# A decode step (attention over a cache, then two small MLP blocks): VectorE's branch removed, one store of four rows, last matrix in pieces of 5, 6, 2 and 1 parts, and the residual's bias prepared earlier

## The chip, the cores and the metric

The kernel runs on one core of a Trainium2 chip. The metric is the device time of one execution in microseconds (us), less is better. The core has five engines that run their own instruction streams side by side: TensorE (PE in the profile; its weight loads are PEld), VectorE (DVE), ScalarE (ACT), GpSimd (POOL) and SyncE (SP). SP and ACT also issue transfers (DMA), which sixteen DMA engines carry out. Engines wait for each other and for transfers through semaphores.

## What is computed

One token of batch 1 with width D = 512 passes an attention over a cache of 16384 positions, with 32 query heads and 8 key/value heads, and then a block B. The reference, cut to what matters:

```python
x = A_x
h = x + _A_ref(_layernorm(x, axis=-1), A_k_cache, A_v_cache, A_wq, A_wo)
h2 = h + _B_ref(_layernorm(h, axis=-1), B_w1, B_w2, B_w3, B_w4)

def _B_ref(x, w1, w2, w3, w4):            # S = 1 here
    h = _gelu(_layernorm(x, axis=-1) @ w1)
    ...                                   # h's four quarters shifted along the sequence by one or two places
    x1 = x + hs
    h2 = _gelu(_layernorm(x1, axis=-1) @ w3) @ w4
    return x1 + h2
```

The sequence has length one, so a shift along it leaves zeros: hs is zero and x1 = x. What remains of block B is a layernorm, w3 (512 x 1792), a gelu, w4 (1792 x 512) and two additions. Because the input of B is itself a layernorm of h, the output is

h + r (h - mean) + gelu(r' (h - mean) @ w3) @ w4

with r the inverse root of the layernorm and r' that of the two layernorms in a row.

## The kernel before

The kernel is written without a scheduler. Each operation is recorded by a helper (`pe`, `dve`, `act`, `pool`, or `P.op` directly) into the list of its engine with the keys it reads (`r`) and writes (`w`); `Program.op` derives the dependences, and `Program.emit` writes each engine's list out in the order in which it was recorded, with a semaphore wait in front of an operation whose dependence is on another engine or a transfer. `emit` calls `_run` for SP, ACT and POOL, `_vector` for VectorE and `_tensor` for TensorE. So the order of the text is the order on each engine.

An operation without a function (`dve(None, ...)`, `pe(None)`) marks a place. `_vector` puts a hint for a branch at VectorE's start (L146), sets a register to 0 (L147), runs the list up to the marked place, waits for what the mark depends on, and issues there a branch that is taken if the register is below zero (L154), which it never is. `_tensor` runs TensorE's list in loops and has such a hint (L221) and a never-taken branch (L336) of its own, at `pe(None)` inside the last matrix.

Transfers are issued on SP by `load` (L458), in this order: wq; four pairs of heads with two key halves (`kb`) of 4 MB and a value tile (`vb`) of 8 MB each; then the matrices of the end. Keys and values are loaded while the pair before is worked on; the matrices of the end take the place of the last key halves, wo in `kb[0]`, w3 and w4 in `kb[1]`. SP issues a load as soon as the tile it overwrites is free.

The end runs as follows. `o_b` (L751) is the attention's output. wo is multiplied as 32 rows r_ (L757) in three pieces, `WO = ((0, 16), (16, 28), (28, 32))`. Ahead of the second piece stand six dummy matmuls, `unread(6)` (L498), whose result nobody reads. `osum` (L762) and `row_sums` give h (`hr`), its square (into `xs`, L518), its transpose `hT`, and on TensorE minus the mean and minus the mean square, which VectorE copies into columns 0 and 1 of the state tile `s` (L524). ACT makes `hc`, the centred h (L771). TensorE multiplies w3 in two pieces (L777) and runs four dummy matmuls. Meanwhile the two inverse roots are iterated, r' on VectorE with `kw` made on ACT (L552), r on POOL (L554 to L560); POOL adds 1 to r in column 13 (L785). Two gelus on ACT (L788) and two transposes on VectorE (L792) give `hcol`, 14 columns. The first transpose also waits for the first piece of w4.

ACT writes the residual into the PSUM bank `h_ps` (L799): `hr` times column 13 plus the bias in column 12, where column 12 is minus the mean times r (L797). TensorE adds the product with w4 on top (L805): 14 parts m with four matmuls each, of 32 columns of weights side by side. w4 comes in four transfers:

```python
W4 = ((0, 4), (4, 9), (9, 13), (13, 14))
```

Part m waits for the transfer that holds it. Finally ACT copies `h_ps` to `fin` (L810), which holds the four quarters of the output row on partitions 0, 32, 64 and 96, and two transfers write it out, two rows each, one issued by SP and one by ACT (L814); SP's last instruction (L816) waits for both.

Of the kernel before, what the change touches and what calls it, by code (L numbers as in the profile page):

```python
# [10 lines left out]
ACTF = mybir.ActivationFunctionType  # L11
# [13 lines left out]
class Program:  # L25
# [69 lines left out]
    def emit(self):  # L95
        for ops in self.ops.values():
            for o in ops:
                for d in o.deps:
                    d.needed = True
        told = {self.place(o) for e in ("PE", "DVE") for o in self.ops[e] if o.needed and o.at}  # L100
        for e in ("PE", "DVE"):
            for o in self.ops[e]:
                o.needed = o.needed or (o.at is not None and self.place(o) in told)
        for e, ops in self.ops.items():
            sems, n = {}, {}
            for o in ops:
                if o.dma is None and o.needed:
                    if o.own not in sems:
                        name = f"e_{e}" if o.own is None else f"e_{e}_{o.own}"
                        sems[o.own] = self.ctx.enter_context(self.nc.semaphore(name))  # L110
                    n[o.own] = n.get(o.own, 0) + o.worth
                    o.sem, o.val = sems[o.own], n[o.own]
        self.nc.switch_bb("body", parent=None)
        for e, eng in (("SP", self.nc.sync), ("ACT", self.nc.scalar), ("POOL", self.nc.gpsimd)):
            self._run(eng, self.ops[e], {})
        self._vector()
        self._tensor()

    @staticmethod
# [15 lines left out]
    def _run(self, eng, ops, have):  # L135
        for o in ops:
# [2 lines left out]
                    eng.wait_ge(s, v)  # L139
                    have[i] = v  # L140
            self._issue(eng, o)

    def _vector(self):
        eng = self.nc.vector
        rv = eng.alloc_register("never")
        hint = eng.mark_branch_hint_location()  # L146
        eng.reg_mov(rv, 0)  # L147
        ops, seen = self.ops["DVE"], {}
        on = next(n for n, o in enumerate(ops) if o.fn is None)
        self._run(eng, ops[:on], seen)  # L150
        for s, v, _ in self._wants(ops[on]).values():
            eng.wait_ge(s, v)

        eng.br_lt(rv, 0, "body", "ve_on").branch_hint(hint)  # L154
        self.nc.switch_bb("ve_on", parent=None)
        self._run(eng, ops[on + 1:], seen)

    def _tensor(self):
        nc, eng, ops = self.nc, self.nc.tensor, self.ops["PE"]
# [191 lines left out]
WO = ((0, 16), (16, 28), (28, 32))  # L351
VP = 2
W3 = ((0, 2), (2, 4))
W4 = ((0, 4), (4, 9), (9, 13), (13, 14))
PAIRS = HKV // 2
RPARTS = 6
QPAD = 4 * 7
# [10 lines left out]
def bass_sequential_preLN__gqa_block_cached__mixer_s_mlp__decode_kernel(  # L368
# [13 lines left out]
    with ExitStack() as ctx:  # L382
        sb = lambda name, shape, dt: ctx.enter_context(nc.sbuf_tensor(name, shape, dt))
        ps = lambda name, shape, dt: ctx.enter_context(nc.psum_tensor(name, shape, dt))
        P = Program(nc, ctx)
# [36 lines left out]
        bias = sb("bias", [128, 1], FP32)  # L422
# [9 lines left out]
        hr = sb("hr", [128, 128], FP32)  # L432
# [50 lines left out]
        def dve(fn, r=(), w=(), bank=()):  # L483
            return P.op("DVE", fn, r, w, bank)

        def act(fn, r=(), w=(), bank=()):
            return P.op("ACT", fn, r, w, bank)
# [8 lines left out]
        def unread(times):  # L496
            field = qb[:, :, :, :].rearrange("p a j q -> p (a j q)")
            P.op("PE", lambda e: e.matmul(O_ps[1][:, :], field[:, 0:128], field[:, 0:512], start=True, stop=True),  # L498
                 r=["qb"], bank=[("O", 1)], times=times)
# [253 lines left out]
        for r_ in range(32):  # L753
            q = r_ % 4
            if r_ == WO[1][0]:
                unread(6)
            pe(lambda e, r_=r_, q=q: e.matmul(O_ps[0][32 * q:32 * q + 32, :], copies(o_b[:, r_:r_ + 1], 32),  # L757
                                              wo_sb[:, r_ * D:(r_ + 1) * D], start=(r_ < 4), stop=(r_ >= 28)),
               r=["o_b"] + [("r", 0, n) for n in (piece(WO, r_),) if n], w=[("O", 0)], bank=[("O", 0)])
# [8 lines left out]
        s = st[1]  # L768
# [6 lines left out]
        for k in range(NCH):  # L775
            for q in range(4):
                pe(lambda e, k=k, q=q: e.matmul(s_ps[32 * q:32 * q + 32, 0, 0:FQ], hc[:, k, :],  # L777
                                                w3_sb[:, k, q * FQ:(q + 1) * FQ], start=(k == 0), stop=(k == NCH - 1)),
                   r=["hc"] + [("r", 1, n) for n in (piece(W3, k),) if n], w=[("s", 0)], bank=[("s", 0)])
        unread(4)  # L780
        variances(1, (0, 1))
        seeds(1, (0, 1))
        inverse_root(1, 1, dve, act)
# [2 lines left out]
        for n in range(2):  # L786
# [5 lines left out]
            dve(lambda e, lo=lo, hi=hi: e.transpose(  # L792
                hcol[:, lo:hi, :].rearrange("p m u -> p (m u)"),
                hg[:, :].rearrange("p (i m) -> p m i", m=NHC)[:, lo:hi, :]), r=[("hg", n)] + [("r", 1, len(W3))] * (n == 0), w=[("hcol", n)])
        dve(None, r=[("r", 1, len(W3) + 1)])

        act(lambda e: e.activation(s[:, 12:13], s[:, 0:1], ACTF.Identity, scale=s[:, 6:7]),  # L797
            r=[(S, 0), (S, 6)], w=[(S, 12)])
        act(lambda e: e.activation(h_ps[:, 0:128], hr[:, :], ACTF.Identity, bias=s[:, 12:13], scale=s[:, 13:14]),  # L799
            r=["hr", (S, 12), (S, 13), ("hcol", 0)], w=[hkey], bank=[hkey])  # L800
        for m in range(NHC):
            if m == W4[1][0]:
                pe(None)
# [4 lines left out]
                   r=[("hcol", 1)] * (2 * m >= NHC) + [("r", 1, len(W3) + n) for n in (piece(W4, m),) if n],  # L808
                   w=[hkey], bank=[hkey], also=[("hcol", 0)] * (2 * m < NHC))
        act(lambda e: e.activation(fin[:, :], h_ps[:, 0:128], ACTF.Identity), r=[hkey], w=["fin"], bank=[hkey])  # L810

        rows = out[0, 0:1, :].rearrange("o (q j) -> (o q) j", q=4)
        for n, by in enumerate(("SP", "ACT")):
            P.op(by, lambda e, n=n: e.dma_start(rows[2 * n:2 * n + 2, :], fin[64 * n:64 * n + 64:32, :]),  # L814
                 r=["fin"], w=[("out", n)], dma=f"out{n}")
        P.op("SP", lambda e: e.nop(), r=[("out", 0), ("out", 1)])  # L816
        P.emit()

    return nc
# [28 lines left out]
```

## Time and profile before

| what | value |
|---|---|
| median of three runs | 190.89 us (190.88 to 191.0) |
| the profiled execution | 190.97 us |
| its span, first to last instruction | 189.53 us |
| bytes read from HBM | 79.17 MB, 418 GB/s over the span |
| busy: PE, DVE, ACT, POOL | 68%, 62%, 8%, 4% of the span |
| mean granted clock of TensorE | 0.887 |

The profile is of one execution. Its parts are the busy times, the span in slices, the DMA queues, the chain of work that ended last (followed back from the last instruction to what released each step), groups of equal instructions with their mean duration and what ended the idle time before them, and the transfers with the time from issue to landing. In a timeline a row gives the start in us, the duration in us, the engine (SPq and ACTq are the issuing sides of SP and ACT), the line, the operation, the tile written and the tiles read, the shapes and the number of instructions merged into the row; in brackets stands the idle time of the engine before it and what ended it. In a row of a DMA queue stand the packets, the MB and the share of the time of sixteen engines. The records behind these views also have each packet's start and each transfer's landing to the nanosecond.

### The profile page before, as it was taken

The page shows a single profiled execution, that of the slowest core. Times are in us where ns is not written, and L with a number is a line of the kernel's source. Part 1 is how long each engine was busy: PE and PEld are TensorE (multiplying, and loading weights), DVE is VectorE, ACT ScalarE, POOL GpSimd, SP SyncE. Part 2 cuts the span into 40 slices and gives each one's busy share as a digit, 9 for nine tenths or more (in the row PEclk, how much of TensorE's full clock was granted, in tenths as well). Part 3 has the DMA queues.
Part 4 walks back from the last instruction along what each step waited for, and adds up shares of the span by engine and source line. Part 5 has one row for each costly group of instructions (what it writes and reads, how often), then busy time and mean ns, then how long its engine had stood idle before and what let it go on. Part 6 is the DMA issues. An engine that isn't in the chain of part 4 may idle for free.

```text
span 189.5 us, 2371 instructions
## 1 busy us (share of the span) xinstructions
PE 128.4 (68%) x743; PEld 48.0 (25%) x743; DVE 117.6 (62%) x151; ACT 14.4 (8%) x23; POOL 6.7 (4%) x15
## 2 busy tenths in 40 slices
PE   0109709996980498968703979696539996974874
PEld 0103203442230133322301423223113332231222
DVE  6740799995523989945038989460469896614270
ACT  3000200000400000004000000040000000500031
POOL 7100000000000000000000000000000000000040
PEclk9999985899999579996995899996978999998755
DMA  6999999999899999997999999999999989999992
GB/s 222 443 443 443 443 443 443 443 443 443 367 415 436 443 553 443 443 443 325 422 443 394 422 429 443 443 443 443 443 436 422 443 387 422 436 429 415 414 410 108
DMA packets 3330, 79.20 MB, mean 418 GB/s; under 512 B 384, under 2 KB 512, under 8 KB 1280
## 3 DMA queue, kind: packets, MB, share of 16 engines
q1 hardware_dynamic: 3316, 79.17, 97.5%
q8 instruction: 1, 0.02, 0.0%
q14 instruction: 1, 0.01, 0.0%
q10 hardware_dynamic: 12, 0.00, 0.0%
HBM read 79.17 MB, written 0.00 MB: 418 GB/s over the span
## 4 chain that ended last, share of the span: by engine, by line
DMA 66%; DVE 15%; PE 14%; issue 3%; SPq 1%; ACT 0%; DVEq 0%
DMA kb<-in_A_k_cache_dram 45%; DMA kb<-in_B_w_dram 14%; DVE kt L635 14%; PE banks L646 9%; DMA vb<-in_A_wq_dram 6%; PE banks L612 5%; SPq L458 1%; DVE qcol L619 1%; PE banks L805 0%; DVE qb L626 0%; DVE xn L603 0%; ACT fin L810 0%; SPq L139 0%; DVEq L139 0%; DVE qn L720 0%
## 5 line engine op out<-in xcount | busy, mean ns | idle before, releaser
L646 PE MATMUL banks<-kt,qn 128*128 x256 | 69.5, 415 | 25.3 <-DVE kt L635 23.9
L635 DVE STREAM_TRANSPOSE kt<-kb 128x2048 int32<-128x2048 int32 (+1 forms) x37 | 71.3, 1989 | 10.0 <-DMA kb<-in_A_k_cache_dram 8.4
L646 PEld LDWEIGHTS banks<-kt,qn 128*128 x256 | 26.3, 103 | 67.9 <-issue 51.8
L498 PE MATMUL banks<-qb 128*128 128x512 bf16 x58 | 22.3, 462 | 0.4
L686 PE MATMUL banks<-vb,pt 128*32 128x512 bf16 x256 | 16.4, 412 | 3.6 <-POOLq L473 2.9
L671 ACT ACTIVATE p_sb<-banks,bias 128x1024 bf16<-128x1024 f32 x4 | 4.5, 1114 | 132.6 <-DVE nmh L667 132.6
L702 DVE TENSOR_SCALAR od<-banks,rowc 128x128 f32<-128x128 f32 x4 | 1.4, 351 | 19.1 <-PE banks L686 19.1
L675 DVE STREAM_TRANSPOSE pt<-p_sb 64x1024 bf16<-64x1024 bf16 x8 | 9.9, 1239 | 5.4 <-ACT p_sb L671 5.3
L612 PE MATMUL banks<-vb,xn 128*128 x32 | 8.7, 440 | 6.1 <-DVE xn L603 6.1
L660 DVE TENSOR_REDUCE mx<-banks 128x1 f32<-128x1024 f32 x4 | 4.9, 1224 | 8.0 <-PE banks L646 8.0
L686 PEld LDWEIGHTS banks<-vb,pt 128*32 128x32 bf16 x256 | 7.0, 103 | 11.2 <-POOLq L473 3.1
L498 PEld LDWEIGHTS banks<-qb 128*128 128x128 bf16 x58 | 5.8, 104 | 15.4 <-issue 15.2
L619 DVE STREAM_TRANSPOSE qcol<-banks 64x1024 f32<-64x1024 f32 x4 | 4.8, 1227 | 6.9 <-PE banks L612 6.9
L554 POOL TENSOR_SCALAR st<-st 128x1 f32<-128x1 f32 x1 | 0.2, 246 | 175.9 <-DVE st L534 175.9
L663 PE MATMUL banks<-mxd,mean 128*128 128x128 f32 x8 | 2.0, 326 | 6.6 <-DVE mxd L661 6.6
L612 PEld LDWEIGHTS banks<-vb,xn 128*128 128x128 bf16 x32 | 3.5, 110 | 10.9 <-issue 8.3
L708 PE MATMUL banks<-od,zo 128*32 128x128 f32 x8 | 1.6, 285 | 6.5 <-DVE od L705 6.5
L655 ACT ACTIVATE banks<-mean 128x1024 f32<-128x1024 f32 x4 | 4.1, 1027 | 18.7 <-DVE qcol L619 18.6
L705 DVE SCALAR_TENSOR_TENSOR od<-banks,rowc,od 128x128 f32<-128x128 f32 x12 | 4.2, 350 | 0.4
L579 PE MATMUL banks<-x,quarter 4*128 4x128 bf16 x1 | 0.3, 284 | 6.0 <-DVE quarter L577 6.0
L576 DVE CAST ident<-ident_f 4x4 bf16<-4x4 f32 x1 | 3.8, 3848 | 0.6 <-POOL ident_f L571 0.6
L762 DVE COPY osum<-banks 128x256 f32<-128x256 f32 x2 | 0.8, 420 | 5.2 <-PE banks L757 5.2
(77 smaller groups left out, 45.6 us busy)
## 6 DMA issues: line engine op xcount, KB each, us to landing
kb<-in_A_k_cache_dram SPq DMA_DIRECT2D x8, 4096.0 KB, 29.7
vb<-in_A_v_cache_dram SPq DMA_DIRECT2D x2, 4096.0 KB, 29.5
vb<-in_A_wq_dram SPq DMA_DIRECT2D x1, 4096.0 KB, 12.2
kb<-in_A_wo_dram SPq DMA_DIRECT2D x1, 2048.0 KB, 25.0
kb<-in_B_w_dram SPq DMA_DIRECT2D x2, 896.0 KB, 23.2
kb<-in_A_wo_dram SPq DMA_DIRECT2D x1, 1536.0 KB, 28.3
kb<-in_B_w_dram SPq DMA_DIRECT2D x2, 512.0 KB, 25.9
kb<-in_B_w_dram SPq DMA_DIRECT2D x1, 640.0 KB, 26.0
```

Of the source, the lines that this page charges most:

```text
L498: P.op("PE", lambda e: e.matmul(O_ps[1][:, :], field[:, 0:128], field[:, 0:512], start=True, stop=True), r=["qb"], bank=[("O", 1)], times= ...
L576: dve(lambda e: e.tensor_copy(ident[:, :], ident_f[0:4, 0:4]), r=["ident_f"], w=["ident"])
L612: pe(lambda e, k=k: e.matmul(row[:, bass.ds(P.b + P.b0, 512)], copies(xn[:, k:k + 1], 128), wq_k[:, k, bass.ds(P.c + P.c0, REP * DH)], sta ...
L619: dve(lambda e, g=g, b=b, half=half: e.transpose(qcol[64 * g:64 * g + 64, 2 * b:2 * b + 2, :, :].rearrange("p e m u -> p (e m u)"), half.r ...
L635: P.op("DVE", lambda e, view=view: e.transpose(view(kt), view(kb[y])), r=[("r", y, i) for i in range(RPARTS)], w=[("kt", t + i) for i in r ...
L646: pe(lambda e, n=n: e.matmul(row[:, bass.ds(P.y, 512)], qn[:, n, bass.ds(P.q, 128)], key_piece(P.k, n), start=False, stop=(n == 3), skip_g ...
L655: act(lambda e: e.activation(s_all, copies(mean4[:, 0:1], 1024), ACTF.Identity, scale=0.0), r=["mean4", "p"], w=[("s", 0), ("s", 1)], **both)
L660: dve(lambda e: e.tensor_reduce(mx[:, :], s_all, AX.X, ALU.max), r=[("s", 0), ("s", 1)], w=["mx"], **both)
L671: act(lambda e: e.activation(p_sb[:, :], s_all, ACTF.Exp, bias=bias[:, 0:1], scale=float(SCALE), accum_out=acc[:, :]), r=[("s", 0), ("s", ...
L675: dve(lambda e, g=g: e.transpose(pt[64 * g:64 * g + 64, :, :, g, :], p_sb[64 * g:64 * g + 64, :]), r=["p"], w=["pt"])
L686: pe(lambda e, l=l, ct=ct, ch=ch: e.matmul(O_ps[0][32 * ct:32 * ct + 32, :], pt[:, l, ch, :, :].rearrange("p g u -> p (g u)"), tiles[:, l ...
L705: dve(lambda e, block=block, c=c: e.scalar_tensor_tensor(od[:, :], block, rowc[:, c:c + 1], od[:, :], ALU.mult, ALU.add), r=[key, "rowc", ...
```

## The change

VectorE's list is now written out by `_run` like those of SP, ACT and POOL, without hint, register, final wait and branch; TensorE's branch stays, and its mark moves with the first piece of w4 from part 4 to part 5. w4 comes in pieces of 5, 6, 2 and 1 parts in place of 4, 5, 4 and 1. The dummy matmuls ahead of wo's second piece are five in place of six. ACT makes two things between `hc` and `kw`: the mean (column 0 with its sign turned) in column 12, and the centred h in `xs`, which is free by then. The residual is then `xs` times column 13 plus column 12, (h - mean)(1 + r) + mean, the same value as before; the bias no longer depends on r. One transfer on SP stores the four rows of `fin`, and SP's last instruction waits for it.

```diff
@@ emit
-        for e, eng in (("SP", self.nc.sync), ("ACT", self.nc.scalar), ("POOL", self.nc.gpsimd)):
+        for e, eng in (("SP", self.nc.sync), ("ACT", self.nc.scalar), ("POOL", self.nc.gpsimd),
+                       ("DVE", self.nc.vector)):
             self._run(eng, self.ops[e], {})
-        self._vector()
         self._tensor()
@@
-    def _vector(self):
-        eng = self.nc.vector
-        rv = eng.alloc_register("never")
-        hint = eng.mark_branch_hint_location()
-        eng.reg_mov(rv, 0)
-        ops, seen = self.ops["DVE"], {}
-        on = next(n for n, o in enumerate(ops) if o.fn is None)
-        self._run(eng, ops[:on], seen)
-        for s, v, _ in self._wants(ops[on]).values():
-            eng.wait_ge(s, v)
-
-        eng.br_lt(rv, 0, "body", "ve_on").branch_hint(hint)
-        self.nc.switch_bb("ve_on", parent=None)
-        self._run(eng, ops[on + 1:], seen)
@@
-W4 = ((0, 4), (4, 9), (9, 13), (13, 14))
+W4 = ((0, 5), (5, 11), (11, 13), (13, 14))
@@ wo
-                unread(6)
+                unread(5)
@@ behind w3's matmuls
         unread(4)
+        act(lambda e: e.activation(s[:, 12:13], s[:, 0:1], ACTF.Identity, scale=-1.0), r=[(S, 0)], w=[(S, 12)])
+        act(lambda e: e.activation(xs[:, :], hr[:, :], ACTF.Identity, bias=s[:, 0:1], scale=1.0), r=["hr", (S, 0)], w=["xs"])
         variances(1, (0, 1))
@@ behind the transposes
-        dve(None, r=[("r", 1, len(W3) + 1)])
-
-        act(lambda e: e.activation(s[:, 12:13], s[:, 0:1], ACTF.Identity, scale=s[:, 6:7]),
-            r=[(S, 0), (S, 6)], w=[(S, 12)])
-        act(lambda e: e.activation(h_ps[:, 0:128], hr[:, :], ACTF.Identity, bias=s[:, 12:13], scale=s[:, 13:14]),
-            r=["hr", (S, 12), (S, 13), ("hcol", 0)], w=[hkey], bank=[hkey])
+
+        act(lambda e: e.activation(h_ps[:, 0:128], xs[:, :], ACTF.Identity, bias=s[:, 12:13], scale=s[:, 13:14]),
+            r=["xs", (S, 12), (S, 13), ("hcol", 0)], w=[hkey], bank=[hkey])
@@ the store
-        rows = out[0, 0:1, :].rearrange("o (q j) -> (o q) j", q=4)
-        for n, by in enumerate(("SP", "ACT")):
-            P.op(by, lambda e, n=n: e.dma_start(rows[2 * n:2 * n + 2, :], fin[64 * n:64 * n + 64:32, :]),
-                 r=["fin"], w=[("out", n)], dma=f"out{n}")
-        P.op("SP", lambda e: e.nop(), r=[("out", 0), ("out", 1)])
+        P.op("SP", lambda e: e.dma_start(out[0, 0:1, :].rearrange("o (q j) -> (o q) j", q=4), fin[0:128:32, :]),
+             r=["fin"], w=["out"], dma="out")
+        P.op("SP", lambda e: e.nop(), r=["out"])
```

## The prediction

> **What bounds the kernel now.** I read the page's own chain of waits first, then that chain in order of time from 157 us on, then the timeline of the last stage, then the DMA records of two windows, and last the landing of each transfer in the trace.
>
> ```profile
> span 189.5 us, 2371 instructions
> DMA 66%; DVE 15%; PE 14%; issue 3%; SPq 1%; ACT 0%; DVEq 0%
> ```
>
> Two thirds of the chain that ended last is DMA. The records of the window from 2 to 186.4 us, and of the window after it, show why:
>
> ```profile
> q1 hardware_dynamic: 3302, 78.84, 99.6%
> ...
> q8 instruction: 1, 0.02, 1.6%
> q14 instruction: 2, 0.02, 1.1%
> ```
>
> In the first window the sixteen DMA engines are 99.6% busy, with SP's loads and nothing else (it has only that queue). The two instruction queues appear only behind the last weight packet. So no edit ahead of 186 us can gain anything unless it takes bytes off the loads, and any byte put onto a DMA engine is paid at the end. The change can act on the last weights' landing, and on what lies between it and the last instruction. The chain there:
>
> ```profile
> 159.71 26.85 DMA kb<-in_B_w_dram
> 186.56 0.04 issue
> 186.61 0.75 PE banks L805 x20
> 187.36 0.02 issue
> 187.38 0.28 ACT fin L810
> ```
>
> The third piece of w4 (parts 9 to 12) lands at 186.56, then 20 matmuls, then the copy to `fin`. The timeline of the same stretch, with what feeds it:
>
> ```profile
> 177.20 1.25 PE L757 MATMUL banks<-kb,o_b 128*32 128x512 bf16 x16
> ...
> 181.58 0.20 ACT L552 ACTIVATE st<-st 128x1 f32<-128x1 f32 x1
> ...
> 182.79 0.27 DVE L558 TENSOR_SCALAR st<-sti,st 128x1 f32<-128x1 f32 x1
> ...
> 183.94 1.04 DVE L792 STREAM_TRANSPOSE hcol<-hg 128x224 bf16<-128x224 bf16 x2 [0.68 <-ACT hg L788]
> 184.24 0.30 ACT L797 ACTIVATE st<-st 128x1 f32<-128x1 f32 x1
> 184.29 0.23 POOL L785 TENSOR_SCALAR st<-st 128x1 f32<-128x1 f32 x1
> 184.63 0.46 ACT L799 ACTIVATE banks<-hr,st 128x128 f32<-128x128 f32 x1
> 185.15 1.15 PE L805 MATMUL banks<-kb,hcol 128*32 128x128 bf16 x36
> 186.61 0.72 PE L805 MATMUL banks<-kb,hcol 128*32 128x128 bf16 x20 [0.31 <-DMA kb<-in_B_w_dram]
> 187.38 0.28 ACT L810 ACTIVATE fin<-banks 128x128 bf16<-128x128 f32 x1 [2.29 <-PE banks L805]
> 187.68 0.60 SPq L814 DMA_DIRECT2D out_dram<-fin  x1
> 187.69 0.56 ACTq L814 DMA_DIRECT2D out_dram<-fin  x1
> ```
>
> TensorE starts w4 at 185.15 with nine parts in hand and then stands until the third piece comes; ACT and DVE have been done for over a microsecond. The transfers' landings in the trace, in us: wo's second and third pieces 176.73 and 178.00, w3's second 182.38, w4's four 183.67, 185.25, 186.56, 186.84. The stores: SP's, issued 187.684, landed 189.239; ACT's, issued 187.689, landed 189.504; the span ends at 189.527, when SP's wait for the second of them ends. One execution of 190.97 us thus has a span of 189.53 and 1.44 around it; it is 0.08 above the median of 190.89.
>
> **The pieces of w4.** The bytes, the number of transfers (four) and of descriptors stay, so the last part, alone in its piece in both kernels, should land at 186.84 again. Before, 16 matmuls wait for 186.56 and run from 186.608; they go out in groups of eight some 0.107 apart (186.608, 186.689, then 186.796 and 186.903 by the trace), so the last part's four come at 187.009 to 187.019 although it has been there since 186.84. After, only parts 11 and 12, eight matmuls, stand on the third piece, and are out by about 186.70. The last four then start when their own piece lands: 186.84 plus the 0.044 that the first of 186.608 took after 186.564, so 186.884 to 186.895. That is 0.124 earlier, and the first matmuls after a pause take 0.287 where one in a stream takes 0.311 to 0.314, so 0.14 to 0.15. I take 0.14. The second piece now carries parts 5 to 10 and lands some 0.65 ahead of 186.56 (two parts of a piece whose four took 1.31), at 185.91; its 24 matmuls need three groups of eight, 0.32, and are out by 186.3, before the third piece comes. The first piece grows to five parts and lands at 183.67 + 1.58 / 5 = 183.99; VectorE's first transpose waits for it and started at 183.94, so it moves to about 184.03, and the start at 185.15 by less than 0.1. What covers this is the stand of TensorE: 44 matmuls need 0.6, so the start may slip to 186.0. Bounds: 0 if the last piece lands as late as TensorE gets to it now, 0.3 if one dummy matmul less (below) lifts the granted clock, 0.50 over this stretch, and the last 0.31 shrinks by half.
>
> **The one store.** ACT's issue (0.56) goes, and SP's final wait is for one landing in place of two. By SP's own two-row store the landing comes 1.555 after the issue, by ACT's 1.815, and the longer sets the end now: 0.265 less. Four rows have no row of their own as a store; the load of x is four rows of the same 256 bytes: 1.357 after its issue, its rows spread over 0.11 (1.969 to 2.080), where SP's two rows were 0.008 apart. I take SP's row, plus half that spread for two rows more: 1.615, a gain of 0.20. Bounds: 0 (as ACT's) and 0.46 (as the load of x). I stay at the store, since reading and writing ends differ for a load.
>
> **The bias known ahead.** ACT's `activation` of 0.30 at 184.24 behind POOL's 184.20 goes from the late chain; two others come between `hc` (ends 181.47) and `kw` (181.58): about 0.20 as L552 and 0.40 as `hc`. `kw` ends near 182.3 instead of 181.78; VectorE wants it at 182.79 and POOL makes its own. The addition to h_ps still waits for POOL's last value (184.52) and for the first transpose (about 184.55), so it starts at about 184.6 as now. Nothing on the path; without that cover 0.6.
>
> **One dummy matmul less (L498, five for six).** Each is 0.43. TensorE is free 0.4 earlier at 176.8, where wo's second piece has just landed (176.73), but the third comes at 178.00 and starts the last four of wo as now. Worth 0, as the loads set every later start up to w3's second half.
>
> **VectorE's branch.** Gone are the hint (0.05) and the register move (0.04) at 0.75 us, in front of a wait for wq that lands at 12.9, and at 185.28 a wait and a 0.07 branch behind which VectorE does nothing more. TensorE's own branch stays, four matmuls later. As instructions: 0. But two instruction transfers follow the two branches (TensorE's at 185.236, VectorE's at 185.280): 16 KB at 186.483 for 0.927, and 8 KB at 187.120 for 0.307. If the branch or its hint is what held one of them back, it may now go among the loads. Bounds: 0, and the 0.93. I take 0, since VectorE's some 170 instructions go once straight through and no instruction transfer of any engine is seen among the loads; the trace doesn't say whose these two are.
>
> [...]
>
> **Sum.** 190.97 - 0.14 - 0.20 = 190.63; less the 0.08 by which this execution stands above the median, **190.55**, 0.18% below 190.89. A difference of about 0.2%, 0.38 us (190.51, 191.27), is what a measurement of this kernel can tell from no change.
>
> **Rivals.**
> Code among the loads (the slower side). Place: one of the sixteen engines, any time from 2 to 186 us. They never idle, and their order at landing stays from wq (12.42 to 12.92) to the last piece (186.34 to 186.84), so a lag of one engine stays to the end. Price: 16 KB at the loads' pace (4 KB in 0.161 to 0.165) is 0.65, alone it took 0.93. On a middle engine (186.56) that ends 0.37 to 0.65 past 186.84, on the last by all of it: 190.92 to 191.48, say 191.2. It decides from a shift of 0.34 on. For it: both transfers come right behind the two branches. Against: nothing shows that VectorE needs a block; one of 8 KB (0.32) would cost the middle engine 0.04 only.
> A store as quick as x's load, since it no longer shares its issue with another: 0.46 for 0.20, so 190.29. For it: SP's first packet came 1.20 after its issue, x's 0.94. Against: x shared its start with wq's load too.
> Half the gain only: the store's four rows land as late as ACT's two, or TensorE's last four matmuls are as late as now: 190.55 + 0.14 to 0.20, 190.7. Against: the landing at 186.84 and the issue of 187.684 are plain in the trace.
> A change that does less than it says: the piece of parts 11 and 12 is issued before the last one as the third was, so nothing speaks for this beyond the case before.
>
> **How the numbers follow.** Forecast (190.40 to 190.65) 0.46, code among the loads 0.28, quick store 0.15, half the gain 0.11. Faster by over 0.2%, below 190.51: a little under half of the forecast, all of the quick store: 0.38. Slower, above 191.27: somewhat over half of the code case: 0.18. The rest, 0.44, within 0.2%. The range takes in the quick store's better half and the code case up to a middle engine: 190.25 to 191.30, with some 0.04 left below and 0.15 above.
>
> **What would show it.** After: third piece near 186.56 with eight matmuls behind it, last piece 186.84, the last four near 186.88, `fin` near 187.24, SP's issue near 187.55, one landing some 1.6 later, span near 189.19. The code case is wrong if the instruction queues again appear only behind the loads; right if one appears before 186 us and the last landing moves past 186.84. A later start of w4 than 186.0, or a `kw` later than 182.79, would make the covers wrong.

## The result, and the profile after

The changed kernel takes 191.67 us (median of nine runs, 191.24 to 191.81) and the kernel before, in the same comparison, 190.88 (nine runs, 190.55 to 191.07): a ratio of 1.0039, with a 95% interval of 1.0031 to 1.0048. It is 0.79 us slower. 190.55 was predicted, with a range of 190.25 to 191.30.

The profiled execution of the changed kernel took 191.74, 0.77 more than that of before, with 1.42 around its span in place of 1.44. Its page still has DMA as two thirds of the chain that ended last:

```profile
span 190.3 us, 2359 instructions
DMA 66%; DVE 14%; PE 14%; issue 4%; SPq 1%; ACT 0%; DVEq 0%
```

The DMA records from 2 to 186.4 us, the window in which before had SP's queue alone, now have a second row (packets, MB, share of the time of sixteen engines):

```profile
q1 hardware_dynamic: 3284, 78.72, 99.4%
q14 instruction: 1, 0.01, 0.0%
```

The stretch from 52 to 53 us shows what it costs by itself. A packet counts whole in the window in which it starts, so a share can pass 100%; 2.0% of sixteen engines over 1 us is 0.32 us of one engine:

```profile
q1 hardware_dynamic: 16, 0.52, 125.4%
q14 instruction: 1, 0.01, 2.0%
```

The packet records give it to the nanosecond: 8192 bytes at 52.299 us for 0.313. The records don't name a packet's engine, but the transfer starts where one packet ends, and a packet of 32 KB starts at 52.605, where the transfer ends (52.612). It took 1.871, where the others that start from 52 to 53 us take 1.213 to 1.216. So by these times one engine lost 0.31 + 0.66 = 0.97 us. Until then the sixteen engines land a transfer within 0.36 to 0.38 us of each other; from the next landing on within 1.25 to 1.33, up to the third piece of w4 (0.50 to 0.56 all through in before). The first of these landings is at 62.234 in place of 61.417, and each later one is some 0.8 late as well, up to w3 and the third piece of w4 (187.33 where 186.56 was forecast). The engine that lands second to last is where it was (0.01 earlier). So it is one engine that is late, and its lag stays; the records show the engines 99.4% busy, which leaves hardly any idle time to make it up in.

The end of the chain, in order of time (start, duration, what):

```profile
161.01 26.95 DMA kb<-in_B_w_dram
187.96 0.04 issue
188.00 0.33 PE banks L789 x3
188.33 0.02 issue
188.35 0.28 ACT fin L794
```

It is now the last piece of w4, one part, that sets the end, not the third as before; it lands at 187.959 in place of 186.840. That is 1.12 late: 0.8 from the engine's lag, and 0.3 more of its own. The timeline of the same stretch:

```profile
184.88 1.04 DVE L779 STREAM_TRANSPOSE hcol<-hg 128x224 bf16<-128x224 bf16 x2 [0.80 <-DMA kb<-in_B_w_dram]
...
185.57 0.46 ACT L783 ACTIVATE banks<-xs,st 128x128 f32<-128x128 f32 x1 [0.55 <-DVE hcol L779]
...
186.09 0.46 PE L789 MATMUL banks<-kb,hcol 128*32 128x128 bf16 x20 [1.22 <-ACT banks L783]
...
186.75 0.92 PE L789 MATMUL banks<-kb,hcol 128*32 128x128 bf16 x32 [0.20 <-DMA kb<-in_B_w_dram]
...
188.00 0.30 PE L789 MATMUL banks<-kb,hcol 128*32 128x128 bf16 x4 [0.33 <-DMA kb<-in_B_w_dram]
188.35 0.28 ACT L794 ACTIVATE fin<-banks 128x128 bf16<-128x128 f32 x1 [2.32 <-PE banks L789]
188.65 0.63 SPq L795 DMA_DIRECT2D out_dram<-fin  x1
```

The last part has its four matmuls alone behind its landing, as the change intends, and `fin` starts 0.394 after the landing, where before it was 0.542. The store is issued at 188.654 and lands at 190.286, 1.632 later, where before the longer of two took 1.815. The two profiled spans close: +1.12 for the landing, -0.15 for what follows it, -0.18 for the store, together +0.79 (190.318 - 189.527). The clock is about the same in both stretches, 0.50 in before and 0.52 from 188.00 to 188.35 us here.

So the two gains of the forecast stand in this profile nearly as sized (0.14 and 0.20), and over a microsecond of late landing, for which the forecast has 0, outweighs them.

### The profile page after: what moved, and what is told of

The parts are those of the page before. It is cut to its first block, busy times and chain, and to the rows that moved or that the text cites. A ratio compares the mean times of both kernels' runs of the same rounds, so it can differ in the third digit from the quotient of the medians.

```text
span 190.3 us, 2359 instructions
## 1 busy us (share of the span) xinstructions
PE 127.2 (67%) x737; PEld 48.1 (25%) x742; DVE 117.6 (62%) x151; ACT 14.4 (8%) x24; POOL 6.7 (3%) x15
## 4 chain that ended last, share of the span: by engine, by line
DMA 66%; DVE 14%; PE 14%; issue 4%; SPq 1%; ACT 0%; DVEq 0%
DMA kb<-in_A_k_cache_dram 46%; DMA kb<-in_B_w_dram 14%; DVE kt L620 13%; PE banks L631 9%; DMA vb<-in_A_wq_dram 6%; PE banks L597 5%; SPq L443 1%; DVE qcol L604 1%; DVE qb L611 0%; PE banks L789 0%; DVE xn L588 0%; ACT fin L794 0%; SPq L139 0%; DVEq L139 0%; DVE qn L705 0%
## 5 line engine op out<-in xcount | busy, mean ns | idle before, releaser
L631 PE MATMUL banks<-kt,qn 128*128 x256 | 70.7, 427 | 23.2 <-DVE kt L620 22.0
L631 PEld LDWEIGHTS banks<-kt,qn 128*128 x256 | 26.8, 105 | 66.6 <-issue 49.8
L671 PE MATMUL banks<-vb,pt 128*32 128x512 bf16 x256 | 18.0, 441 | 3.6 <-POOLq L458 3.0
L483 PE MATMUL banks<-qb 128*128 128x512 bf16 x52 | 18.5, 388 | 0.5
L742 PE MATMUL banks<-kb,o_b 128*32 128x512 bf16 x32 | 3.0, 487 | 3.3 <-DMA kb<-in_A_wo_dram 2.0
```

The lines of the kernel that those rows point to most:

```text
L631: pe(lambda e, n=n: e.matmul(row[:, bass.ds(P.y, 512)], qn[:, n, bass.ds(P.q, 128)], key_piece(P.k, n), start=False, stop=(n == 3), skip_g ...
L671: pe(lambda e, l=l, ct=ct, ch=ch: e.matmul(O_ps[0][32 * ct:32 * ct + 32, :], pt[:, l, ch, :, :].rearrange("p g u -> p (g u)"), tiles[:, l ...
```

## The experiments

Each kernel was run beside the kernel before on the same chip; in five groups, in which before had medians of 190.80, 190.78, 190.70, 190.61 and 190.67. The span is the mean over a kernel's executions, and so is the time outside the span (before: 189.3 to 189.5, and 1.33 to 1.35).

| kernel | edit | median | ratio [95%] | span | outside |
|---|---|---|---|---|---|
| branch_out | before without VectorE's branch | 191.64 | 1.0043 [1.0031, 1.0055] | 190.23 | 1.35 |
| branch_kept | changed, VectorE's branch kept | 190.87 | 1.0002 [0.9992, 1.0011] | 189.24 | 1.64 |
| no_hint | before, branch kept, hint out | 191.40 | 1.0030 [1.0019, 1.0041] | 190.11 | 1.33 |
| nops20 | changed, 20 empty operations | 191.49 | 1.0035 [1.0022, 1.0047] | 190.16 | 1.33 |
| pad20 | changed, 20 small memsets early, tile in front | 191.31 | 1.0023 [1.0013, 1.0033] | 189.84 | 1.38 |
| two_fetches | changed, 66 memsets, tile in front | 191.23 | 1.0028 [1.0019, 1.0038] | 189.89 | 1.36 |
| two_fetches_b | the same, tile behind | 192.20 | 1.0085 [1.0069, 1.0100] | 190.80 | 1.40 |
| pad_only | changed, unused tile in front | 190.65 | 1.0004 [0.9994, 1.0014] | 189.35 | 1.35 |
| early_mark | before, branch ahead of o_f | 190.88 | 1.0007 [0.9998, 1.0016] | 189.49 | 1.37 |
| late_mark | before, branch behind the last piece | 191.82 | 1.0056 [1.0042, 1.0071] | 189.40 | 2.43 |
| kept_early | branch_kept, branch a piece earlier | 191.57 | 1.0041 [1.0029, 1.0052] | 190.18 | 1.35 |
| two_stores | kept_early with two stores | 190.89 | 1.0011 [1.0003, 1.0020] | 189.57 | 1.35 |
| one_store | before with one store | 190.49 | 0.9988 [0.9980, 0.9997] | 189.18 | 1.34 |
| pieces | before with the new pieces | 190.86 | 1.0013 [1.0003, 1.0023] | 189.45 | 1.50 |
| one_store_five | one_store, third piece cut in two | 190.61 | 1.0000 [0.9991, 1.0009] | 189.34 | 1.33 |
| pad_before | before, unused tile in front | 190.09 | 0.9965 [0.9951, 0.9978] | 188.78 | 1.33 |
| one_store_pad | one_store, unused tile in front | 190.03 | 0.9960 [0.9946, 0.9973] | 188.66 | 1.34 |

### The branch alone, and all but the branch

branch_out does one part of the change alone, the first hunk of its diff with the mark behind the transposes taken out too. branch_kept undoes that part alone. no_hint leaves branch, register and wait in the kernel before and takes out what points ahead to it:

```diff
-        hint = eng.mark_branch_hint_location()
@@
-        eng.br_lt(rv, 0, "body", "ve_on").branch_hint(hint)
+        eng.br_lt(rv, 0, "body", "ve_on")
```

> Kernel before with VectorE's hint, register, final wait and branch taken out, nothing else. Theory (code among the loads): the 8 KB instruction transfer comes near 52 us as in the changed kernel, holds its DMA engine up by about 0.97 us (0.31 for itself, 0.66 for the transfer behind it), the last piece of w4 lands near 187.8 to 188.0 where it landed at 186.84, and the time is before plus 0.9 to 1.1: 191.8 to 192.0. Rival (the store, the pieces or the bias make the changed kernel slower): no instruction transfer ahead of 186 us, 190.9.

> Changed kernel with VectorE's branch left in as before; store, pieces, bias and dummy matmuls as changed. Theory: no instruction transfer ahead of 186 us, last piece near 186.84, the gains of 0.14 (pieces) and 0.2 (store) come through: 190.4 to 190.65. Rival: 191.5 or more.

> Kernel before with the branch left in, but without its hint at the start. If the hint is what holds the code transfer back: 8 KB near 52 us, 191.8 to 192.0. If the branch alone holds it: none ahead of 186 us, 190.9.

The branch alone explains the loss: taking it out costs 0.84 (191.64 to 190.80), keeping it in the changed kernel takes it to 0.07 of before. Its size was a little less than the 0.9 to 1.1 expected of branch_out, and in the execution that was profiled, the shortest of the six (191.15), the last piece landed at 187.36 and not at 187.8 to 188.0. There too the transfer took 0.325 and the packet behind it 1.875. But the spread of the landings was 0.73 to 0.77 ahead of the transfer and is 0.97 behind it, so only about 0.24 of the engine's lag reached the end. How much does reach it depends on where the engine stands among the sixteen: in the changed kernel the spread grows by 0.90 (0.37 to 1.27), in no_hint by all of the 0.97 (0.67 to 1.64). The DMA records from 2 to 186.4 us, of branch_out and then of branch_kept:

```profile
q1 hardware_dynamic: 3285, 78.83, 99.6%
q14 instruction: 1, 0.01, 0.0%
```

```profile
q1 hardware_dynamic: 3297, 78.77, 99.4%
```

The row of q14 is there in the one and missing in the other, so these 8 KB are VectorE's code. no_hint has the transfer too, 8192 bytes at 52.631, and costs 0.60 with the branch still in place (191.40, under the 191.8 to 192.0 expected): it is the hint, near VectorE's start, that keeps the code back (with it the first 8 KB come at 187.120 in before). In every trace here row q14 has exactly two transfers of 8 KB behind 20 us: both from 185.9 us on where hint and branch are kept, and the first among the loads where the hint is gone.

branch_kept shows the second thing that the forecast has wrong. It was expected at 190.4 to 190.65 and came at 190.87. Its span did shrink, by 0.23 (189.24 to 189.47), but the time outside it grew by 0.29. The end of its timeline is as early as the forecast has it:

```profile
185.69 1.58 PE L805 MATMUL banks<-kb,hcol 128*32 128x128 bf16 x56
...
187.32 0.28 ACT L810 ACTIVATE fin<-banks 128x128 bf16<-128x128 f32 x1 [1.68 <-PE banks L805]
187.62 0.62 SPq L811 DMA_DIRECT2D out_dram<-fin  x1
```

Its branch runs at 186.03 where that of before ran at 185.28, since the first two pieces of w4 now hold eleven parts in place of nine. Two code transfers of VectorE follow, at 187.587 and at 190.307, and the execution ends after the second of them. That is taken up below.

### Where in the program the code comes

nops20 put 20 empty operations at VectorE's start, pad20 put 20 real ones (memsets of one column of a tile that nobody reads) ahead of `xn`:

```diff
+        pad = sb("pad", [128, 80], FP32)
@@ ahead of xn
+        for i in range(20):
+            dve(lambda e, i=i: e.memset(pad[:, i:i + 1], 0.0))
```

> Changed kernel with 20 instructions that do nothing at VectorE's start. If the transfer comes when VectorE's instruction count reaches the end of a block of code, it comes 20 instructions earlier: near 22 to 27 us for 52.3, the late engine shows first in the landing of 32 us for that of 61 us, and the time stays at 191.5 to 191.8. If it comes at a fixed time or from another engine: again near 52 us.

> The changed kernel with 20 one-column memsets on VectorE ahead of xn, where it waits for wq. If the transfer comes when VectorE's instruction count reaches a block's end, it comes 20 instructions earlier: 26 to 30 us for 52.3, and the late engine shows from the landing of about 32 us on. If it comes at a fixed time or from another engine: again near 52 us. Time 191.4 to 191.7 in both.

nops20 tells nothing of the place: the trace of VectorE has none of its 20 operations, and its first memset starts at 0.81 as in the changed kernel. So it is a second run of the changed kernel, with the transfer at 52.126; whether the operations are in the program at all the trace doesn't say. In pad20 the transfer came earlier, though not as early as the 26 to 30 us expected. The DMA records from 31 to 32 us have it:

```profile
q14 instruction: 1, 0.01, 1.9%
```

It starts at 31.464. Count VectorE's records in the trace, leaving out the second record of an operation that also reads its accumulator: the transfer starts when 60 or 61 of them have started in the changed kernel, nops20, branch_out and no_hint (at 52.1 to 54.4 us), and when 63 have in pad20, of which twenty are the memsets. So the transfer hangs on a position in VectorE's program, not on a time or a load. two_fetches, next, has its second one 126 records behind the first. VectorE's transfers here are 8 KB in every trace (a block, in what follows), and one among the loads cost 0.97 us of an engine in the changed kernel, where the DMA engines are 99.4% busy.

pad20's time, 191.31, is below the 191.4 to 191.7 expected. Its tile stands in front of the tiles of keys and values, which matters by itself, as the next runs show.

### What a second block costs

two_fetches adds 22 such memsets behind each of the first three pairs of heads, which brings a second block among the loads (at 140.130 us, the first at 53.459). two_fetches_b is the same with the tile allocated behind `kt`, so that the tiles of keys and values stay where they were. pad_only has the tile in front and no memsets.

> The changed kernel with 22 one-column memsets on VectorE behind each of the first three pairs, so that its program passes a second block's end among the loads. Theory (each code transfer costs its DMA engine about 0.97, and no idle time of that engine gives it back): a first 8 KB near 52 us, a second near 140 to 150, the latest engine about 1.9 to 2.2 behind the first at the landing of 158 us where the changed kernel has 1.26, the time 0.8 to 1.0 above the changed kernel: 192.4 to 192.6. Rival (the lag is made once, or caught up): 191.5 to 191.7.

> As the run two_fetches (22 one-column memsets on VectorE behind each of the first three pairs of the changed kernel), with their tile allocated behind the key and value tiles. If a transfer's lag adds to the time and the drift came from the shifted tiles: median landings as in the changed kernel up to 140 us, latest engine 2.1 behind the first after it, 0.5 to 0.9 above the changed kernel's 191.67: 192.2 to 192.5. If the other engines take it back: 191.2 to 191.7.

> The changed kernel with a tile of 320 bytes a partition allocated ahead of the key and value tiles and never used. If the shift of the tiles makes the loads drift: median landings up to 0.7 ahead of or behind the changed kernel's at 158 us. If the memsets did it: as the changed kernel within 0.1, 191.5 to 191.7.

two_fetches missed, at 191.23. It has both transfers (53.459 and 140.130), and the time from the first landing engine to the last grows from 0.40 to 1.25 and then to 2.10, as a second block should make it; but the engines gain on those of before by and by, the middle of them by 0.32 us at 129 us and 0.73 at the end. pad_only shows that the tile alone does this: with no memset it is 0.0035 of the time quicker than the changed kernel (1.0004 to 1.0039), its middle engine 0.69 ahead at the end. In two_fetches_b, with the tile out of the way, the middle engine stays within 0.03 of before (but for the two enlarged pieces of w4), and the result is as expected, 192.20. Its DMA records from 2 to 186.4 us, and from 141 to 142 us:

```profile
q1 hardware_dynamic: 3272, 78.73, 99.4%
q14 instruction: 2, 0.02, 0.0%
```

```profile
q14 instruction: 1, 0.01, 2.0%
```

The packets behind its two blocks took 1.868 and 1.875 against 1.213 to 1.215, the same 0.66 as in the changed kernel. The last landing is 0.29 later than in before already ahead of the first block, 0.63 later behind it and 1.61 behind the second: the first block added 0.34 there and the second its full 0.98. In the medians the two cost 1.59 (192.20 to 190.61), twice the 0.79 of the changed kernel.

### What VectorE's code does at the end

In the kernels with the hint transfers of 8 KB come on q14 too, behind VectorE's last instructions: in before at 187.120 and 189.842, with the branch at 185.280. Three kernels move the branch: early_mark ahead of o_f, late_mark behind w4's last piece, and kept_early one piece earlier than branch_kept:

```diff
@@ late_mark
-        dve(None, r=[("r", 1, len(W3) + 1)])
+        dve(None, r=[("r", 1, len(W3) + 3)])
@@ kept_early, from branch_kept
-        dve(None, r=[("r", 1, len(W3) + 1)])
+        dve(None, r=[("r", 1, len(W3))])
```

> The kernel before, with VectorE's branch ahead of the reduction of the attention's output, near 172.5 us, waiting for no weights. Theory (the branch lets the code transfer go, and a transfer among the loads costs its DMA engine about 0.97): 8 KB near 174, the last piece lands at 187.4 to 188.0, 191.3 to 191.9. Rival (only a transfer in the loops costs, or VectorE's branch has nothing to do with the transfer): 190.7 to 190.9.

> The kernel before, with VectorE's branch waiting for the last piece of w4 in place of the second, so at about 186.9 in place of 185.28. Theory (VectorE's code transfers hold the end up): second transfer at about 191.4, 191.7 to 191.9. Rival (VectorE's end is of no account, since it has no work left): 190.8 to 190.95.

> The changed kernel with VectorE's branch, as in the run branch_kept, but its wait is for the first piece of w4 and not for the second (which holds six parts now and lands later). Theory: VectorE's code for the end of the run comes in two transfers one behind the other, the first some 1.5 to 1.8 us after the branch, the second 2.4 us after the first is through, and in branch_kept (branch at 186.0) the second came at 190.31, 1.0 us behind the span's end, and held the end up. With the branch at about 185.5 the second comes at about 189.8, the time outside the span falls from 1.64 to about 1.35, and the 0.23 of span gained show: 190.5 to 190.65. Rival (the time outside the span grew for another reason, the missing store on ACT say): 190.8 to 190.95, outside 1.6.

In early_mark the branch ran at 172.593, but the transfer came at 185.947, behind VectorE's last transpose, which ends at 184.92. So passing the branch early does not let the code go early; the expectation missed and its rival held. In late_mark the span is that of before (189.40), and the time outside it is 2.43 in place of 1.33. The DMA records from 190 to 193 us, after everything that the kernel waits for:

```profile
q14 instruction: 1, 0.01, 1.1%
```

It starts at 191.011, its branch having run at 187.014, and the last semaphore event in the trace is at 191.967. In pieces it starts at 190.003 and the last event is at 190.958; in branch_kept at 190.307, with the last event at 190.977. So the run ends some 0.7 to 0.95 after this second transfer starts, if that is later than span and the usual 1.33 would have it. The first transfer comes 1.55 to 1.56 after the branch in these three kernels, the second 2.4 to 2.7 after the first. Counted from the branch the last event is 4.95 later in all three, though the second transfer is not at a fixed place in between. So what follows the branch on VectorE sets the end there; whether it is the transfer itself is not shown. This is where branch_kept and pieces lose outside the span (1.64 and 1.50): the larger second piece delays the branch.

kept_early was to win that back and came at 191.57. One of its executions took 190.55 (span 189.1), the others 191.4 to 192.0 (spans 190.1 to 190.6), so the loss is inside the span. Waits of SP in it (us in total, times, longest), and then in branch_kept:

```profile
SPq L813 <- DMA out_dram<-fin: 1.9, 1, 1.9
```

```profile
SPq L813 <- DMA out_dram<-fin: 1.0, 1, 1.0
```

Three rows of the store started at 188.805 to 188.826 and landed by 189.207. VectorE's second transfer ran from 188.778 to 189.225; the fourth row started at 189.221 and landed at 190.124. By these times the row waited for the engine that carried the transfer. One row, 0.4 late, lands 0.9 late. Two stores of two rows were to avoid that engine:

```diff
-        P.op("SP", lambda e: e.dma_start(out[0, 0:1, :].rearrange("o (q j) -> (o q) j", q=4), fin[0:128:32, :]),
-             r=["fin"], w=["out"], dma="out")
+        rows = out[0, 0:1, :].rearrange("o (q j) -> (o q) j", q=4)
+        for n, by in enumerate(("SP", "ACT")):
+            P.op(by, lambda e, n=n: e.dma_start(rows[2 * n:2 * n + 2, :], fin[64 * n:64 * n + 64:32, :]),
+                 r=["fin"], w=[("out", n)], dma=f"out{n}")
```

> As the run kept_early (changed kernel, VectorE's branch kept and waiting for w4's first piece), but with the two stores of two rows of the kernel before. Theory (only the fourth row of the single store met VectorE's second code transfer): no row waits behind it, the span is less than that of the kernel before by the pieces' 0.14, outside 1.35: 190.6 to 190.7. Rival (the early branch itself costs): 191.4 to 191.6 again.

They did: 190.89, and no store was held up. The expected 190.6 to 190.7 was missed by 0.2; its mean span is 0.2 above that of before, and no run tells why.

### The gains one at a time

one_store and pieces put one part of the change each into the kernel before. one_store_five adds to one_store `W4 = ((0, 4), (4, 9), (9, 11), (11, 13), (13, 14))`, which frees the last part without delaying the branch.

> The kernel before with one store of four rows on SP, nothing else. Predicted term: 0.20 less span, 0.2 less time (190.6). Theory now: the span gains 0.2, but the fourth row goes through the DMA engine that also carries VectorE's code, so an execution in which VectorE's second code transfer meets it ends 0.7 to 1.0 later: most executions near 190.6, some near 191.5. Rival: 190.6 throughout.

> The kernel before with w4 in pieces of 5, 6, 2 and 1 parts, nothing else; VectorE's branch then waits for a piece of six parts. Predicted term: the last matmuls 0.14 earlier, so a span less by 0.14. Theory now: VectorE's branch comes at 185.9 to 186.0 instead of 185.28, its second code transfer near 190.3 holds the end, outside the span about 1.6: 190.75 to 190.95 in all. Rival: outside unchanged at 1.35, 190.65.

> The kernel before with one store (as the run one_store, 190.49) and w4 in five pieces of 4, 5, 2, 2 and 1 parts, so that VectorE's branch still comes near 185.3 and eight matmuls fewer stand behind the third landing. If TensorE's last matmuls still set the end: 0.05 to 0.15 less than one_store. If at a full granted clock they do not, as the page of one_store suggests (0.335 from the last landing to the copy, 0.33 in the run pieces): the same as one_store within 0.05, or slightly more for the fifth transfer.

The store is worth about what was forecast: the span is 0.19 shorter (189.18 to 189.37), and no execution shows the loss of kept_early (190.40 to 190.71; in the profile the second transfer comes at 189.632, after the store). In the traces with one store it lands 1.62 to 1.64 after its issue, kept_early apart, and the later of two stores 1.815 to 1.865. The interval of the ratio, 0.9980 to 0.9997, still leaves room for a gain from 0.06 to 0.38 us. The pieces are worth nothing: the span is 0.08 longer and the time outside it 0.16. Nor did five pieces gain; in one_store_five, at a ratio of 1.0000, not even the store's gain is seen, and no run tells why. Why the pieces gain nothing shows in the same stretch, 186.4 to 187.3 us, of before, one_store and pieces (busy time of PE, PEld, DVE, ACT and POOL with instructions, then granted clock, DMA share, GB/s):

```profile
186.40:187.30 0.90, 0.69 (x20) 0.46 (x20) 0.00 (x0) 0.00 (x0) 0.00 (x0) 0.50 0.09 27
```

```profile
186.40:187.30 0.90, 0.56 (x20) 0.34 (x20) 0.00 (x0) 0.00 (x0) 0.00 (x0) 1.00 0.14 31
```

```profile
186.40:187.30 0.90, 0.67 (x24) 0.22 (x12) 0.00 (x0) 0.00 (x0) 0.00 (x0) 1.00 0.08 23
```

In the profile of before TensorE has half its clock there (0.50), in the other two all of it (1.00). At the full clock the old pieces get from the last landing to `fin` in 0.337 (one_store) and the new ones in 0.335 (pieces). The other traces agree. Of the eight kernels with the old four pieces six need 0.334 to 0.337, all at the full clock; only before (0.542) and one_store_pad (0.484) have half of it there. Of the ten with the new pieces seven need 0.334 to 0.337, and the changed kernel, nops20 and pad_only 0.391 to 0.395. So the 0.14 is seen only between executions that end at about half the clock (0.542 in before, 0.394 in the changed kernel), and before's profile happened to be one of them.

### A kernel that beats both

pad_before and one_store_pad have the unused tile of 320 bytes per partition ahead of the tiles of keys and values, and no other edit:

```diff
+        pad = sb("pad", [128, 80], FP32)
```

> The kernel before with the unused tile of 320 bytes a partition ahead of the key and value tiles, nothing else. If the shift is a gain of its own: median landings 0.6 to 0.7 ahead at the end, 189.9 to 190.1. If it only makes up for the code transfer: 190.6 to 190.8.

> The kernel before with one store (run one_store: 0.2 less) and the unused tile. If both gains add and VectorE's second code transfer comes behind the store: 189.7 to 189.95. If it meets the fourth row: about 190.6.

The tile takes the kernel before to 190.09 (0.9965, interval 0.9951 to 0.9978), all of it in the span; its last piece lands at 186.362 in place of 186.840. With the one store it is 190.03, the best of the kernels run, a little above what was expected. The 0.06 to pad_before is less than these runs can tell, so the store's 0.2 is not seen a second time here either.

## Why the prediction was wrong, point by point

**The bound was read right.** The DMA engines are 99.4 to 99.6% busy, and the last landing sets the end. "Any byte put onto a DMA engine is paid at the end" held for the engine that carried the 8 KB; the end of the run saw of it what reached past the engine that was last anyway (0.24 in branch_out's profile, 0.90 in the changed kernel's). That only fewer bytes can gain ahead of 186 us is not so: with the unused tile in front the same loads end at 186.362 in place of 186.840 (pad_before).

**VectorE's branch: the step that failed.** The forecast has "I take 0, since VectorE's some 170 instructions go once straight through and no instruction transfer of any engine is seen among the loads". The absence was an effect of the hint that the change removes (without it alone, in no_hint, 8 KB come at 52.631), not a fact about VectorE's length: in the changed kernel the first transfer comes at the 60th of VectorE's 168 records, long before its list is through. The rival "code among the loads" was the right mechanism, on the right side, at 0.28. Its price was too low. It has 0.32 for 8 KB and 0.04 at the end on a middle engine; the transfer took 0.31, but with the 0.66 on the packet behind it the engine lost 0.97. It stood close to last, and against before 0.8 of that reached the end. Another 0.3 came on the last piece: its last write, of 4 bytes, began at 187.185, and the landing followed 0.774 later in place of 0.465, and VectorE's next code transfer began at 187.191, right behind it. In nops20, pad20 and pad_only too the spread of the landings grows by about 0.3 at the last piece; in those four the code starts right behind that write. In branch_out (0.98, then 0.97) and no_hint, where it starts 0.35 or more later, and in the two kernels with both blocks among the loads, which have none there, the spread doesn't grow. That the code causes this 0.3 was not tried by itself. The rival's "both transfers come right behind the two branches" pointed the right way, though it is the hint and not the branch that holds the code (no_hint), and passing the branch does not release it (early_mark).

**The pieces of w4: right in the profile, not in the kernel.** 0.14 was forecast and the two profiles show 0.15, both of them at about half the clock. The single edit shows no gain (span +0.08). The term was worked out of durations at a granted clock of 0.50 and carried to executions that needn't have it: that the two profiles met it was luck; it also had no price for the branch that comes 0.7 later, which puts 0.16 (pieces) to 0.29 (branch_kept) outside the span where the branch is kept and waits for the larger second piece.

**The one store: right.** Forecast 1.615 after its issue and 0.20 of gain; measured 1.632, and 0.19 of span alone, in one comparison. What was not foreseen is that its fourth row can start behind VectorE's code (in kept_early at 189.221, where the other three started by 188.826).

**The bias known ahead and the dummy matmul: right at 0.** The covers held, though one sign that was named against them came: w4 starts at 186.09, later than 186.0. That follows the late engine, since the first piece lands 0.8 later than was forecast (184.78 for 183.99); in branch_kept, without the lag, w4 starts at 185.69. These are the rows of the changed kernel, ACT's new two, then `kw`, then VectorE's operation that needs it:

```profile
182.21 0.19 ACT L766 ACTIVATE st<-st 128x1 f32<-128x1 f32 x1
182.30 0.39 ACT L767 ACTIVATE xs<-hr,st 128x128 f32<-128x128 f32 x1
182.59 0.19 ACT L537 ACTIVATE st<-st 128x1 f32<-128x1 f32 x1
...
183.61 0.27 DVE L543 TENSOR_SCALAR st<-sti,st 128x1 f32<-128x1 f32 x1
```

`kw` is done 0.8 before it is wanted. The residual at 185.57 waits for the transpose, as the timeline's brackets show, which waits for w4's first piece.

**The sum.** In medians, the branch is +0.84, the store -0.21, and the pieces with the rest of the change about 0: +0.6, of the measured 0.79. The difference is about the accuracy of three such comparisons. Whether the 0.3 on the last piece is part of it stays open: of branch_out only the shortest execution was profiled, and the others may have it.

## What to carry to other kernels

A hint or a branch that does nothing to the computation can still decide when an engine's code is fetched (the first 8 KB of VectorE at 187.120 us with the hint, at 52.631 without); where the DMA engines are as busy as here (99.4%), look for such transfers among the loads and at how many instructions lie between them (126 records of VectorE in two_fetches), and price one by what it does to the packet behind it (0.66 us here) and not by its own duration (0.31) alone. An absence in a trace ("no code among the loads") counts for a changed kernel only if the change leaves its cause alone. Before a tenth of a microsecond is worked out of one stretch of one execution, look at the granted clock of that stretch (0.50 in before, 1.00 in one_store and pieces), and try the edit alone.

## What the runs showed of the hardware that was not expected

- A transfer of 8 KB took 0.31 us of a DMA engine and made the 32 KB packet behind it 0.66 longer (1.87 for 1.21), in the changed kernel and at both blocks of two_fetches_b alike. With the tile in front it was 0.53 (1.744 to 1.746 in pad_only and two_fetches). Why is open.
- 320 bytes per partition allocated in front of the tiles of keys and values made the same loads quicker: 0.9965 of the time (0.9951 to 0.9978) in the kernel before. Which tile's place does it was not tried, and pad20, which has the tile too, took 191.31 where pad_only took 190.65; why is open.
- A late branch at the end of VectorE's list held the end of the run: 2.43 us outside the span in place of 1.33 (late_mark). Two code transfers follow it, and the last event comes 4.95 after the branch.
- The 16 KB transfer at the end comes 1.0 to 1.6 us behind TensorE's never-taken branch in every trace, wherever VectorE's branch is and also without it. That points to TensorE's code; a kernel without TensorE's branch was not tried.
